# Second attention layer: the residual added by an accumulating DMA, more rows normalised by ScalarE

## The chip, the cores and the metric

The kernel runs on one NeuronCore of a Trainium2 chip. The engines work side by side, each through its own instructions in program order, and wait for one another through semaphores: TensorE (PE) multiplies matrices into PSUM, VectorE (DVE) and ScalarE (ACT) work element by element, GpSimd (POOL) does the rest, and SyncE (SP) issues transfers. The metric is the device time of one execution in microseconds; the kernel before takes 428.71 us (median of 3 runs, 428.61 to 428.74).

## The reference

Four residual layers run one after the other on x with 2048 positions of 512 features in bf16: attention, convolution, attention, convolution. The change touches the second attention.

```python
def _layernorm(x, axis=-1, eps=1e-5):
    m = jnp.mean(x, axis=axis, keepdims=True)
    v = jnp.var(x, axis=axis, keepdims=True)
    return (x - m) / jnp.sqrt(v + eps)

def _A_ref(x, wqkv, wo):          # 32 heads of 16; window W = 8 keys, dilation 2
    ...
    logits = jnp.einsum("bhsd,bhswd->bhsw", q, kg) * scale
    attn = _softmax(logits, axis=-1)
    o = jnp.einsum("bhsw,bhswd->bhsd", attn, vg)
    return o.transpose(...).reshape(B, S, D) @ wo

x = x + _A_ref(_layernorm(x), A_wqkv, A_wo)
x = x + _B_ref(_layernorm(x), ...)      # long convolution by way of the FFT
x = x + _A_ref(_layernorm(x), A_wqkv, A_wo)   # the layer of the change
x = x + _B_ref(_layernorm(x), ...)
```

So after the attention each position needs x plus the projected output, and then the mean and variance of this sum over 512 features, for the normalisation ahead of the last layer.

## The kernel before

The position s is 16*p + a: p is the partition, a is one of 16 "rows", each a tile of 128 partitions by 512 features. x lives in SBUF as `x_sb[128, 16, 512]`, bf16. The attention's second half is a loop of 16 iterations n, over the rows in the order 0, 2, 1, 3, 4, ... 15. What each engine does in it:

```python
def pv_mult(n):                       # VectorE: attention weights times the 8 values
    nc.vector.tensor_tensor(pv[:], attn..., vap, ALU.mult)          # L404, tile pav, 128x4096
def pv_sum(n):                        # TensorE: sum over the window and transpose
    ... 32 matmuls of pav by ident into po                          # L412
    nc.scalar.copy(oT[:], po[:])                                    # L415

def out_proj(a):                      # TensorE: residual and projection in one PSUM tile
    oT = oTs.pop(a)
    pw = pq_tile()
    xr = x_sb[:, a, :]
    nc.tensor.matmul(pw[:], lhsT=ident[:], rhs=xr, start=True, stop=False)                    # L422
    for ftp in range(NDT):
        nc.tensor.matmul(pw[:], lhsT=oT[:, ftp, :], rhs=self.wo[:, ftp, :], start=False, ...) # L424
    if a >= 12:
        if a >= 14 and l == 1:
            row_stats(nc, lnst, pw[:], a, "dve")
        nc.scalar.copy(xr, pw[:])                                                             # L428
    else:
        nc.scalar.activation(xr, pw[:], ACT.Identity, accum_out=lnst["s1"][:, a:a + 1])       # L430
        row_sumsq(nc, lnst, xr, a)                 # ScalarE: Square, summed into s2            L108
```

The loop, in program order (l is 1 in the second attention layer; parts for the softmax of later rows are cut):

```python
for n in range(16):
    pv_mult(rows[n])
    ...                                      # n = 0, 8: mx; n = 2, 10: recip; n = 4, 11: norm_p
    if n in (1, 3, 5, 7):
        mult(3, n // 2)                      # VectorE, last products of queries and keys
    if n in (7, 11, 15):
        u_begin(n - 7, n - 3, "act", "act" if n > 7 else "pool")
    if n in (8, 12):
        u_end(n - 8)                         # VectorE: bias nb = -mean * rstd                  L148
    if n in (9, 10, 13, 14):
        b0 = 0 if n < 11 else 4
        r0 = b0 + (0 if n in (9, 13) else 2)
        u_apply(b0, range(r0, r0 + 2))       # even rows ScalarE (L158), odd rows VectorE (L160)
    if n == 15:
        x_stats(12)                          # VectorE: bn_stats of a row                       L101
    ...
    pv_sum(rows[n])
    if n == 15:
        x_stats(13)
        u_end(8)
        u_apply(8, range(8, 12), "dve")
    if n > 0:
        out_proj(rows[n - 1])
    ...
u_begin(12, 15, "dve", "act"); out_proj(15)
self.warm(pw, 10, ...)                       # ten matmuls that keep TensorE busy
u_begin(15, 16, "dve", "act"); u_end(12); ...  # rows 12 to 15 normalised, the next layer begins
```

`u_begin` of four rows turns their sums into the reciprocal standard deviation:

```python
mean, ms = lnst["s1"][:, a0:a1], -1.0 / D
nc.vector.scalar_tensor_tensor(msq[:], mean, -1.0 / (D * D), mean, ALU.mult, ALU.mult)              # L133
nc.vector.scalar_tensor_tensor(veps[:], lnst["s2"][:, a0:a1], 1.0 / D, msq[:], ALU.mult, ALU.add)   # L135
if rs == "act":
    return rstd_act(...)                     # ScalarE: Ln with bias EPS (L118), then Exp (L119)
nc.vector.tensor_scalar(rstd[:], var, EPS, None, ALU.add)                # L140
nc.gpsimd.tensor_tensor(rstd[:], rstd[:], lnst["mh"][:, 0:n], ALU.pow)   # L141
```

The tiles `pav`, `oT`, `po` and `pq` have two buffers each. At the front of this layer the mean and variance of x are already computed once, for the normalisation ahead of it (`bn_aggr` into a tile `agg[b]`).

Of the kernel before, what the change touches and what calls it, by code (L numbers as in the profile page):

```python
# [10 lines left out]
ACT = mybir.ActivationFunctionType  # L11
ALU = mybir.AluOpType
AX = mybir.AxisListType
PSUM = bass.MemoryType.PSUM
F32 = mybir.dt.float32
BF16 = mybir.dt.bfloat16
# [4 lines left out]
P = 128  # L21
S = 2048
D = 512
# [3 lines left out]
NA = 16  # L27
NDT = 4
# [70 lines left out]
def row_stats(nc, lnst, x_row, a, eng):  # L99
    if eng == "dve":  # L100
        nc.vector.bn_stats(lnst["bn"][:, a, 0, :], x_row)  # L101
    else:
        nc.scalar.activation(lnst["junk"][:], x_row, ACT.Identity, accum_out=lnst["s1"][:, a:a + 1])
        row_sumsq(nc, lnst, x_row, a)


def row_sumsq(nc, lnst, x_row, a):
    nc.scalar.activation(lnst["junk"][:], x_row, ACT.Square, accum_out=lnst["s2"][:, a:a + 1])  # L108
# [7 lines left out]
def rstd_act(nc, pool, var):  # L116
    rstd = pool.tile(list(var.shape), F32, name="ln_rstd")
    nc.scalar.activation(rstd[:], var, ACT.Ln, bias=EPS)  # L118
    nc.scalar.activation(rstd[:], rstd[:], ACT.Exp, scale=-0.5)  # L119
    return rstd  # L120


def ln_begin(nc, pool, lnst, a0, a1, eng, rs="pool"):
    n = a1 - a0
    if eng == "dve":
        ag = pool.tile([P, n, 2], F32, name="ln_ag")
        for a in range(n):
            nc.vector.bn_aggr(ag[:, a, :], lnst["bn"][:, a0 + a, 0, :])
        var, mean, ms = ag[:, :, 1], ag[:, :, 0], -1.0
    else:  # L130
        mean, ms = lnst["s1"][:, a0:a1], -1.0 / D
        msq = pool.tile([P, n], F32, name="ln_msq")
        nc.vector.scalar_tensor_tensor(msq[:], mean, -1.0 / (D * D), mean, ALU.mult, ALU.mult)  # L133
        veps = pool.tile([P, n], F32, name="ln_veps")
        nc.vector.scalar_tensor_tensor(veps[:], lnst["s2"][:, a0:a1], 1.0 / D, msq[:], ALU.mult, ALU.add)  # L135
        var = veps[:]
    if rs == "act":
        return rstd_act(nc, pool, var), mean, ms
    rstd = pool.tile([P, n], F32, name="ln_rstd")
    nc.vector.tensor_scalar(rstd[:], var, EPS, None, ALU.add)  # L140
    nc.gpsimd.tensor_tensor(rstd[:], rstd[:], lnst["mh"][:, 0:n], ALU.pow)  # L141
    return rstd, mean, ms
# [20 lines left out]
class LayerA:  # L163
# [143 lines left out]
    def core(self, x_sb, u, lnp, ev=None, nprod=0):  # L307

        tc, nc, lnst, l = self.tc, self.nc, self.lnst, self.layer
        ident, nident = self.c["ident"], self.c["nident"]  # L310
# [11 lines left out]
        with ExitStack() as c2:  # L322
# [7 lines left out]
            wk = c2.enter_context(tc.tile_pool(name=f"a{l}_wk", bufs=2, reuse_waits="tile"))  # L330
# [9 lines left out]
            def pq_tile():  # L340
                return ps_q.tile([P, 512], F32, name="pq", tag="pq")
# [76 lines left out]
            def out_proj(a):  # L418
                oT = oTs.pop(a)
                pw = pq_tile()  # L420
                xr = x_sb[:, a, :]
                nc.tensor.matmul(pw[:], lhsT=ident[:], rhs=xr, start=True, stop=False)  # L422
                for ftp in range(NDT):
                    nc.tensor.matmul(pw[:], lhsT=oT[:, ftp, :], rhs=self.wo[:, ftp, :], start=False, stop=(ftp == NDT - 1))  # L424
                if a >= 12:
                    if a >= 14 and l == 1:
                        row_stats(nc, lnst, pw[:], a, "dve")
                    nc.scalar.copy(xr, pw[:])  # L428
                else:
                    nc.scalar.activation(xr, pw[:], ACT.Identity, accum_out=lnst["s1"][:, a:a + 1])  # L430
                    row_sumsq(nc, lnst, xr, a)

            def x_stats(a):
                row_stats(nc, lnst, x_sb[:, a, :], a, "dve")

            def u_begin(a0, a1, eng, rs="pool"):
                lns[a0] = ln_begin(nc, lnp, lnst, a0, a1, eng, rs)
# [11 lines left out]
            def u_end(a0):  # L449
                lns[a0] = ln_end(nc, lnp, lns[a0])  # L450

            def u_apply(a0, rows, eng=None):
                rstd, nb = lns[a0]
                for a in rows:
                    ln_apply(nc, u[:, :, a, :], x_sb[:, a, :].rearrange("p (q r) -> p q r", r=4), rstd, nb, a - a0,
                             eng or ("dve" if a % 2 else "act"))
# [45 lines left out]
            rows = [0, 2, 1, *range(3, NA)]  # L502
            for n in range(16):
                pv_mult(rows[n])
                if n in (0, 8):
                    mx(2 + n // 8)
                if n in (2, 10):
                    recip(2 + n // 8)
                if n in (4, 11):
                    norm_p(2 + n // 8)  # L510
                if n in (1, 3, 5, 7):
                    mult(3, n // 2)
                if n in (7, 11, 15):
                    u_begin(n - 7, n - 3, "act", "act" if n > 7 else "pool")
                if n in (8, 12):
                    u_end(n - 8)
                if n in (9, 10, 13, 14):
                    b0 = 0 if n < 11 else 4
                    r0 = b0 + (0 if n in (9, 13) else 2)
                    u_apply(b0, range(r0, r0 + 2))  # L520
                if n == 15:
                    x_stats(12)
                event(("p", n))
                if n in (1, 3, 5):
                    q_proj(3, n // 2 + 1)
                pv_sum(rows[n])
                if n in (0, 8):
                    sub_exp(2 + n // 8)
                if n == 15:
                    x_stats(13)  # L530
                    if l == 1:
                        u_end(8)
                        u_apply(8, range(8, 12), "dve")
                if n > 0:
                    out_proj(rows[n - 1])
                if n in (1, 3, 5, 7):
                    lsum(3, n // 2)
                event(("o", n))
# [7 lines left out]
            pw = pq_tile()  # L546
# [729 lines left out]
def kernel(  # L1276
# [16 lines left out]
    nc = tc.nc  # L1293
# [6 lines left out]
    with tc.tile_pool(name="ctmp", bufs=1) as tmp:  # L1300
        consts = build_a_consts(tc, nc, cpool, tmp)
    lnst = dict(s1=cpool.tile([P, NA], F32, name="ln_s1"), s2=cpool.tile([P, NA], F32, name="ln_s2"),
                bn=cpool.tile([P, NA, 2, 6], F32, name="ln_bn"), junk=cpool.tile([P, D], BF16, name="ln_junk"),
                mh=cpool.tile([P, 4], F32, name="ln_mh"))
# [12 lines left out]
    xpool = ctx.enter_context(tc.tile_pool(name="xres", bufs=1))  # L1317
    lnp = ctx.enter_context(tc.tile_pool(name="ln_small", bufs=3, reuse_waits="tile"))
    lnst["bn"] = xpool.tile([P, NA, 2, 6], F32, name="ln_bn2")
    x_sb = xpool.tile([P, NA, D], BF16, name="x_sb")  # L1320
# [56 lines left out]
    with tc.manual_schedule(engines=MAN):  # L1377
        la.front_open()
        ln, agg, pts = {}, {}, {}

        def front_pools():
            fb.swap_psum()
            la.front_psum()

        def aggr(b):
            agg[b] = lnp.tile([P, 4, 2], F32, name="ln_ag")
            for a in range(4):
                nc.vector.bn_aggr(agg[b][:, a, :], lnst["bn"][:, 4 * b + a, :, :])

        def power(b):  # L1390
            ln[b] = rstd_act(nc, lnp, agg[b][:, :, 1]), agg[b][:, :, 0], -1.0

        def norm(b):
            la.front_apply(b, x_sb[:, b * 4:(b + 1) * 4, :], ln_end(nc, lnp, ln[b]), ["dve"] * 4)

        def transposes(b):
            pts[b] = la.front_t(b)

        def last(*ops):
            def f():  # L1400
                for op, *ix in ops:
                    front[op](*ix)
            return f

        front = dict(S=front_pools, h=lambda g, t: half_stats(nc, lnst, x_sb, t, g), a=aggr, p=power, n=norm, T=transposes,
                     E=lambda b, d, eng: pts[b][d](eng), P=lambda b, ft: la.front_k(b, ["act"] * 4, (ft,)),
                     Q=lambda q, ft: la.qproj1(q, ft, la.qT[q], la.ps_pj, la.pj_tag), x=lambda b: la.front_ext(b, "dve"),
                     e=lambda ft: la.front_ext(3, "dve", ft))
        fb.run(ORDERF, None, more=front)
        la.front_close()  # L1410
        fb.c_ps.close()
        fb.c_grp.close()
        krctx.close()
        ev = {("p", 8): [lambda: la.load_w2(w2_dram)]}
        ev["m", 0, 0] = [last(("P", 3, 0), ("P", 3, 1), ("x", 0), ("x", 2), ("P", 3, 2), ("Q", 0, 1), ("e", 0), ("Q", 0, 2))]
        ev["m", 0, 1] = [last(("e", 1), ("e", 2))]
        ev["m", 0, 2] = [last(("e", 3))]
        ev["q", 0, 0] = [last(("P", 3, 3), ("Q", 0, 3))]
        la.core(x_sb, u, lnp, ev)
# [51 lines left out]
```

## Time and profile before

| what | value |
|---|---|
| time | 428.71 us |
| span of the profiled execution | 426.7 us |
| VectorE products `pav`, one | 2.284 us, 32 in the kernel, 16 in this layer |
| row loop of the second attention | VectorE's first `pav` at 314.9 us, its last from 364.96 us |
| statistics and bias of the last rows | 367.2 to 374.6 us |
| first TensorE step of the last layer | 375.3 us |

In the profile, L-numbers are lines of the kernel. A line of the timeline has the start in us from the span's start, the duration, the engine, line and operation, the tile written and those read, and in brackets how long the engine sat idle before it and for whom. Times of instructions overlap a little, because an engine takes up the next before the last has drained; so the cost of an instruction in a full stretch is the step from its start to the next start. A view of stretches gives the busy time of each engine between two times.

### The profile page before, as it was taken

To read this page: it belongs to the slowest core of one execution; us is meant where nothing else is said; L and a number is where in the kernel's file an instruction comes from. 1 tells how busy PE (TensorE), PEld (TensorE's weight loads), DVE (VectorE), ACT (ScalarE), POOL (GpSimd) and SP (SyncE) were. 2 spreads that over 40 slices of the span, in tenths; PEclk is the share of its full clock that TensorE was granted. 3 is DMA by queue.
4 is the path that set the end of the run, shared out by engine and by line. 5 is a ranking of instruction groups with operands and counts; after the bars stand their busy time and mean duration, and the time that the engine had idled before them with its cause. 6 is when DMAs were issued, how large, how long until landed. Compare 5 with 4: busy or idle time off the path is not lost.

```text
span 426.7 us, 12737 instructions
## 1 busy us (share of the span) xinstructions
PE 354.2 (83%) x5506; PEld 265.2 (62%) x5506; DVE 395.0 (93%) x537; ACT 323.1 (76%) x554; POOL 43.9 (10%) x46
## 2 busy tenths in 40 slices
PE   3000169999999899999998999999998999997894
PEld 2000127667765687767887898555566777776793
DVE  8999999999999999996999949899999999889864
ACT  6999999986455389887999988755556668689961
POOL 3000300000598000001300000000000020000000
PEclk9999998999999899999999999999999999999999
DMA  8930732132116743572244692810141066416315
GB/s 217 395 103 12 82 78 69 33 68 59 24 40 188 245 109 102 178 298 102 76 175 177 222 322 59 261 56 2 38 111 28 2 229 224 141 55 181 118 40 160
DMA packets 62466, 54.16 MB, mean 127 GB/s; under 512 B 33893, under 2 KB 50890, under 8 KB 61130
## 3 DMA queue, kind: packets, MB, share of 16 engines
q1 hardware_dynamic: 62266, 53.22, 40.6%
q8 instruction: 43, 0.70, 0.8%
q10 hardware_dynamic: 144, 0.13, 0.3%
q14 instruction: 13, 0.11, 0.1%
HBM read 30.28 MB, written 13.24 MB: 102 GB/s over the span
## 4 chain that ended last, share of the span: by engine, by line
PE 46%; DVE 22%; ACT 7%; DMA 4%; issue 3%; SPq 2%; DVEq 0%; ACTq 0%
PE po L412 9%; DVE t L805 5%; DVE pav L404 5%; PE pq L351 4%; PE pk L1165 4%; PE pq L424 4%; DVE a1s L745 4%; PE pp L1103 4%; PE L L302 4%; DVE prod L295 3%; PE pp L242 3%; PE pq L185 3%; PE pb L831 2%; PE pb L832 2%; DMA kf_ring<-kf_dram 1%
## 5 line engine op out<-in xcount | busy, mean ns | idle before, releaser
L404 DVE TENSOR_TENSOR pav<-attn,v_ext 128x4096 bf16<-128x4096 bf16 x32 | 73.0, 2283 | 0.4 <-DMA v_ext<-v_ext 0.4
L412 PEld LDWEIGHTS <-pav 128*128 128x128 bf16 x1024 | 60.0, 99 | 11.1 <-DVE pav L404 7.5
L412 PE MATMUL po<-ident,pav 128*128 128x128 bf16 x1024 | 64.0, 222 | 3.1 <-DVE pav L404 2.8
L295 DVE TENSOR_TENSOR prod<-qT,kT_ext 128x4096 bf16<-128x4096 bf16 x29 | 66.4, 2308 | 0.2
L1093 PE MATMUL pt<-ident,x_blk 128*128 128x128 bf16 x64 | 6.7, 258 | 43.2 <-ACT x_blk L158 43.2
L1005 DVE TENSOR_TENSOR A_t<-A_t,pow_t 128x1024 bf16<-128x1024 bf16 (+4 forms) x46 | 38.3, 873 | 0.2
L1093 PEld LDWEIGHTS <-x_blk 128*128 128x128 bf16 x64 | 5.5, 119 | 46.0 <-ACT x_blk L158 44.0
L818 ACT CAST ub<-pb 128x1024 bf16<-128x1024 f32 x32 | 32.5, 1062 | 1.3 <-DVE t L805 1.1
L353 ACT CAST v_ext<-pq 128x512 bf16<-128x512 f32 x32 | 18.7, 586 | 19.3 <-PE pq L351 18.1
L424 PE MATMUL pq<-wop,oT 128*128 128x512 bf16 x128 | 32.9, 379 | 0.0
L302 PEld LDWEIGHTS <-prod 128*128 128x128 bf16 x928 | 27.1, 96 | 8.8 <-DVE prod L295 3.2
L415 ACT CAST oT<-po 128x512 bf16<-128x512 f32 x32 | 18.5, 579 | 18.2 <-PE po L412 18.0
L1103 PE MATMUL pp<-xnT,kT_ext 128*128 128x512 bf16 x96 | 27.9, 421 | 4.5 <-ACT qT L1108 2.6
L831 PE MATMUL pb<-Wp,t 128*128 128x128 bf16 x256 | 30.2, 219 | 1.8 <-ACT ub L818 0.8
L763 PE MATMUL pb<-a1s,w_sb 128*128 128x64 bf16 x768 | 27.7, 193 | 4.8 <-ACT ub L818 3.5
L351 PE MATMUL pq<-wv,xnT 128*128 128x512 bf16 x128 | 30.7, 379 | 0.0
L745 DVE CAST a1s<-pb 128x1024 bf16<-128x1024 f32 x22 | 26.1, 1217 | 4.9 <-PE pb L756 4.8
L832 PE MATMUL pb<-WpJ,t 128*128 128x128 bf16 x256 | 30.0, 219 | 0.4 <-DVE t L805 0.4
L763 PEld LDWEIGHTS <-w_sb 128*128 128x128 bf16 x768 | 24.8, 98 | 7.5 <-issue 5.9
L302 PE MATMUL L<-ind,prod 128*128 128x8 bf16 x928 | 27.4, 166 | 1.3 <-DVE prod L295 1.1
L745 ACT CAST a1s<-pb 128x1024 bf16<-128x1024 f32 x26 | 25.6, 1043 | 2.0 <-PE pb L756 2.0
L832 PEld LDWEIGHTS <-t 128*128 128x128 bf16 x256 | 24.9, 98 | 3.0 <-issue 1.6
(227 smaller groups left out, 861.1 us busy)
## 6 DMA issues: line engine op xcount, KB each, us to landing
w_sb<-w_dram SPq DMA_DIRECT2D x8, 1024.0 KB, 8.3
w_dram<-w_zero SPq DMA_DIRECT2D x1, 4096.0 KB, 15.5
kf_ring<-kf_dram SPq DMA_DIRECT2D x13, 256.0 KB, 3.6
kf_ring<-kf_dram SPq DMA_DIRECT2D x26, 128.0 KB, 3.6
v_ext<-v_ext SPq DMA_DIRECT2D x4, 784.0 KB, 6.6
x_blk<-in_A_x_dram SPq DMA_DIRECT2D x4, 512.0 KB, 4.1
kT_ext<-in_A_wqkv_dram SPq DMA_DIRECT2D x4, 512.0 KB, 10.8
x_sb<-in_A_x_dram SPq DMA_DIRECT2D x4, 512.0 KB, 4.9
```

Of the source, the lines that this page charges most:

```text
L295: nc.vector.tensor_tensor(pr, self.qT[q][:, ft].unsqueeze(1).to_broadcast([P, W, 4, P]), kap, ALU.mult)
L302: self.nc.tensor.matmul(L[:, al, w, ft * 8:(ft + 1) * 8], lhsT=pr[:, w, al, :], rhs=self.c["ind8"][:], start=(ft == 0 and w == 0 and al % ...
L351: nc.tensor.matmul(pp[:], lhsT=xnT[:, dt, a * P:(a + 1) * P], rhs=wv[:, dt, :], start=(dt == 0), stop=(dt == NDT - 1))
L404: nc.vector.tensor_tensor(pv[:], attn[:, n % 4].unsqueeze(2).to_broadcast([P, W, DH, H]), vap, ALU.mult)
L412: nc.tensor.matmul(po[:, ft, :], lhsT=pvf[:, w, ft * P:(ft + 1) * P], rhs=ident[:], start=(w == 0 and ft == 0), stop=(w == W - 1), skip_gr ...
L424: nc.tensor.matmul(pw[:], lhsT=oT[:, ftp, :], rhs=self.wo[:, ftp, :], start=False, stop=(ftp == NDT - 1))
L745: (self.nc.scalar.copy if eng == "act" else self.nc.vector.tensor_copy)(dst, src)
L763: nc.tensor.matmul(p2[:, j, :], lhsT=self.w2[:, ec * EC + j, :], rhs=a1s[:, ec * EC + j, :], start=True, stop=True)
L831: nc.tensor.matmul(p3[:, j, :], lhsT=t1[:, dql, :], rhs=wp_r, start=True, stop=False)
L832: nc.tensor.matmul(p3[:, j, :], lhsT=t2[:, dql, :], rhs=wpj_r, start=False, stop=True)
L1005: return lambda: nc.vector.tensor_tensor(*args)
L1103: nc.tensor.matmul(pps[kind, b, ft][:], lhsT=la.wqk[:, dt, c:c + P], rhs=la.xnT[:, dt, b * 512:(b + 1) * 512], start=(dt == 0), stop=(dt = ...
```

## The change

For rows 0 to 11 of the second attention layer, the residual is no longer added by TensorE. ScalarE moves the projected output from PSUM to a bf16 tile `ow` of two buffers and sums it on the way, and GpSimd's queue adds `ow` to the row of `x_sb` in a DMA. The sum of squares reads the row after that, so it is taken two iterations later. The sum of a row is now that of the output plus 512 times the old mean of x, which is kept from the front of the layer in `mean0`. Rows 1, 3, 5 and 7 are normalised by ScalarE, no longer by VectorE, and the first `u_begin` takes its power by ScalarE's Ln and Exp instead of GpSimd. The purpose is to take work from TensorE and VectorE and to use GpSimd's queue, which is free.

```diff
@@ ln_begin
         mean, ms = lnst["s1"][:, a0:a1], -1.0 / D
+        if "mean0" in lnst:
+            nc.vector.scalar_tensor_tensor(mean, lnst["mean0"][:, a0:a1, 0], float(D), mean, ALU.mult, ALU.add)
         msq = pool.tile([P, n], F32, name="ln_msq")
@@ out_proj
-                nc.tensor.matmul(pw[:], lhsT=ident[:], rhs=xr, start=True, stop=False)
+                by_dma = l == 1 and a < 12
+                if not by_dma:
+                    nc.tensor.matmul(pw[:], lhsT=ident[:], rhs=xr, start=True, stop=False)
                 for ftp in range(NDT):
-                    nc.tensor.matmul(pw[:], lhsT=oT[:, ftp, :], rhs=self.wo[:, ftp, :], start=False, stop=(ftp == NDT - 1))
-                if a >= 12:
+                    nc.tensor.matmul(pw[:], lhsT=oT[:, ftp, :], rhs=self.wo[:, ftp, :],
+                                     start=(by_dma and ftp == 0), stop=(ftp == NDT - 1))
+                if by_dma:
+                    ow = wk.tile([P, D], BF16, name="ow")
+                    nc.scalar.activation(ow[:], pw[:], ACT.Identity, accum_out=lnst["s1"][:, a:a + 1])
+                    nc.gpsimd.dma_start(xr, ow[:], accum_op=ALU.add)
+                elif a >= 12:
@@ the loop
                 if n in (7, 11, 15):
-                    u_begin(n - 7, n - 3, "act", "act" if n > 7 else "pool")
+                    u_begin(n - 7, n - 3, "act", "act" if n > 7 or l else "pool")
...
-                    u_apply(b0, range(r0, r0 + 2))
+                    u_apply(b0, range(r0, r0 + 2), "act" if l else None)
...
                 if n > 0:
                     out_proj(rows[n - 1])
+                if l == 1 and 3 <= n < 15:
+                    row_sumsq(nc, lnst, x_sb[:, rows[n - 3], :], rows[n - 3])
@@ the front of the second attention layer
+        mean0 = xpool.tile([P, NA, 2], F32, name="ln_mean0")
...
-            agg[b] = lnp.tile([P, 4, 2], F32, name="ln_ag")
+            agg[b] = mean0[:, 4 * b:4 * b + 4, :]
...
+        lnst["mean0"] = mean0
```

## The prediction

> **What bounds the kernel now.** I began with the page's table of busy time by engine.
>
> ```profile
> PE 354.2 (83%) x5506; PEld 265.2 (62%) x5506; DVE 395.0 (93%) x537; ACT 323.1 (76%) x554; POOL 43.9 (10%) x46
> ```
>
> VectorE leads, but the change touches one stage only, the row loop of the second attention layer. By the timeline its first attention product `pav` starts at 314.9 us and the next layer's first TensorE step at 375.3. So I cut that stage into stretches (columns: stretch, its length, then busy us and count of PE, PEld, DVE, ACT, POOL, then clock, DMA share, GB/s).
>
> ```profile
> 323.00:347.00 24.00, 22.88 (x361) 17.97 (x359) 23.74 (x17) 14.29 (x37) 1.73 (x1) 1.00 0.06 14
> 347.00:357.00 10.00, 9.75 (x122) 7.11 (x120) 9.90 (x12) 7.90 (x19) 1.16 (x1) 1.00 0.93 392
> 357.00:371.00 14.00, 13.97 (x183) 11.02 (x183) 12.61 (x18) 10.09 (x26) 0.00 (x0) 1.00 0.37 115
> ```
>
> VectorE fills the first two stretches, TensorE the third, and ScalarE has room on average (14.3 of 24 us, 7.9 of 10, 10.1 of 14). An average hides bursts, so next I read ScalarE's timeline for iterations n = 10 and 11 (columns: start, duration, instruction, idle before it).
>
> ```profile
> 353.94 0.60 ACT L430 ACTIVATE x_sb<-pq 128x512 bf16<-128x512 f32 x1 [0.47 <-PE pq L424]
> 354.44 0.20 ACT L430 ACTIVATION_READ_ACCUMULATOR x_sb<-pq 128x1 f32 x1
> 354.66 0.63 ACT L108 ACTIVATE ln_junk<-x_sb 128x512 bf16<-128x512 bf16 x1
> ...
> 355.83 0.80 ACT L158 ACTIVATE xnT<-x_sb,ln_nb,ln_rstd 128x512 bf16<-128x512 bf16 x1
> 356.54 0.56 ACT L415 CAST oT<-po 128x512 bf16<-128x512 f32 x1
> 357.00 0.59 ACT L430 ACTIVATE x_sb<-pq 128x512 bf16<-128x512 f32 x1
> 357.49 0.20 ACT L430 ACTIVATION_READ_ACCUMULATOR x_sb<-pq 128x1 f32 x1
> 357.72 0.63 ACT L108 ACTIVATE ln_junk<-x_sb 128x512 bf16<-128x512 bf16 x1
> 358.26 0.19 ACT L108 ACTIVATION_READ_ACCUMULATOR ln_junk<-x_sb 128x1 f32 x1
> ```
>
> The reader is to see that ScalarE runs back to back through n = 10 (only 0.47 us idle before n = 9's eviction), and that L108, the sum of squares that follows the eviction of row 9, ends only at 358.45. Steps from start to start: eviction 0.72, sum of squares 0.63, one normalised row 0.71, `oT` 0.46. VectorE at the same time, and at the loop's end:
>
> ```profile
> 357.37 0.15 DVE L133 SCALAR_TENSOR_TENSOR ln_msq<-ln_s 128x4 f32<-128x4 f32 x1
> 357.56 0.16 DVE L135 SCALAR_TENSOR_TENSOR ln_veps<-ln_s,ln_msq 128x4 f32<-128x4 f32 x1
> 357.64 2.28 DVE L404 TENSOR_TENSOR pav<-attn,v_ext 128x4096 bf16<-128x4096 bf16 x1
> ...
> 367.42 0.16 DVE L135 SCALAR_TENSOR_TENSOR ln_veps<-ln_s,ln_msq 128x4 f32<-128x4 f32 x1
> 367.50 0.69 DVE L101 BATCH_NORM_STATS2 ln_bn<-x_sb 128x6 f32<-128x512 bf16 x1
> 369.40 0.69 DVE L101 BATCH_NORM_STATS2 ln_bn<-x_sb 128x6 f32<-128x512 bf16 x1 [1.22 <-ACT x_sb L428]
> ```
>
> L135 (`veps`) reads the sums of squares of four rows, and stands in VectorE's order ahead of the next `pav`. It now waits for nothing, because its rows were squared two iterations earlier. At the end, row 12's and row 13's statistics follow it.
>
> **What the Trainium skill says.** "DMA: Bandwidth & Descriptors", section "SWDGE vs HWDGE vs iDMA": accumulating in a DMA can only be issued from GpSimd; this case's queues of before are hardware and instruction queues only, so the trace has no such transfer. The section "Anatomy of one DMA — SWDGE (gpsimd) path" of the same page fits 2.0 us plus bytes over 436 GB/s; for a row of 128 KB that is an estimate of 2.3 us, to which reading the destination adds something it doesn't give. "SBUF — State Buffer", section "Who interferes with whom": a VectorE operation with two SBUF inputs holds GpSimd's reads out, but, inferred there, not the writing of descriptors. The first half agrees with the trace: GpSimd's power of 4 columns took 2.89 us from 345.27, through the `pav` of 345.00 and into the reduction of 347.31. The second half nothing here shows.
>
> **The change part by part.** (1) TensorE loses one identity matmul for each of 12 rows. In the timeline L422 starts at 361.77 and L424 at 361.99, so 0.22 us each, 2.6 in all; but until 357 TensorE follows `pav`, so only those of its late, full stretch could count. (2) VectorE loses four normalised rows in n = 9, 10, 13, 14, at 0.33 us from start to start (350.73 to 351.05), 1.3 in all, and gains three operations of four columns at 0.19, 0.6 in all, of which one takes the place of adding epsilon at n = 7. (3) ScalarE gains four normalised rows, 4 x 0.71 = 2.8 us, two each in n = 9 to 10 and 13 to 14, plus Ln and Exp at n = 7. (4) The sum of squares of row n-3 now runs after row n-1's eviction, two iterations later than before, so that the DMA has time; its consumer `veps` stays where it was. This is what decides, I think.
>
> First I follow the chain to n = 11. Nothing in VectorE's order changes up to 348.5. At n = 7 `veps` needs row 3, squared at n = 6, about 344.5 by the same steps: just in time. ScalarE from n = 8: `oT` 349.3, the exponential 349.8 (1.03), eviction of row 7 350.8, squares of row 5 351.5, two normalised rows from 352.2, `oT` 353.6, eviction of row 8 354.0, squares of row 6 354.75, Ln and Exp of the reciprocal 355.4, two rows from 355.9, `oT` 357.3, eviction of row 9 357.8, squares of row 7 from 358.5 to 359.25. VectorE, relieved of two rows, would have `veps` of rows 4 to 7 at 357.56 - 0.66 + 0.19 = 357.1; it has to wait until 359.3. The `pav` of n = 12 starts at 359.4 instead of 357.64, **1.75 us late**. Even in ScalarE's old pace its slot ends at 358.45, so a delay of about 0.9 is certain in this order.
>
> Then to the end. `pav` of n = 12 ends at 361.6; TensorE takes 1.79 us for each row's `po` sum and 0.86 (rows below 12) or 1.08 for the projection. ScalarE: evicts row 11 at 364.5, squares row 9 365.2, two rows from 365.85, `oT` 367.25, copies row 12 367.7 (0.5), squares row 10 368.2, two rows from 368.9, `oT` 370.3, copies row 13 370.75, squares row 11 371.25 to 371.98. TensorE alone would give row 13 at 370.0 and so the squares at 371.5. Only then can `veps` of rows 8 to 11 run, at 372.03, and in VectorE's order rows 12 and 13 follow: statistics at 372.11 and 372.73, the latter against 369.40 before. What comes after it keeps its length: bias, four normalised rows, statistics of row 14, its copy, ten warming matmuls, the first step of the next layer. The stage ends **3.3 us later** (372.73 - 369.40). From there VectorE and ScalarE are busy nearly throughout (13.4 and 13.5 of 14 us from 376 to 390), so I carry the shift whole: 428.71 + 3.3 = 432.0 us.
>
> **Rivals.** *TensorE and VectorE are relieved, and it pays.* If the squares came in time, `pav` of n = 12 would start 0.47 us earlier (0.66 less 0.19), and TensorE, full from there, would save one more identity matmul: about 0.7 us, 428.0 us. For it speak the full engines of the stretches; against it that ScalarE, which takes up the work, has no gaps left exactly in n = 9 to 10. *The transfer becomes the wait.* On my chain row 7 is evicted by 351.5 and squared at 358.5, row 8 354.7 and 361.2; the eviction of row 9 into the two-buffer tile needs row 7's transfer 6.3 us after issue. So 6 us are hidden, against an estimated 2.3 plus something. The stretch 347 to 357 moves 392 GB/s for the next layer's weights at a DMA share of 0.93, and there it might take 5 to 7 us; at 8 us each wait adds up to 2 us, 434 to 436. *GpSimd's issue slows VectorE* through shared access: the same DMA page, section "Latency and other measured facts", gives about 1 us from a GpSimd issue to the first byte, so 12 issues could cost some 10 us as an estimate, 440 us; in the trace all 32 `pav` take 2.27 to 2.29 us, also the one beside GpSimd's power, which speaks against it.
>
> **Range and chances.** The delay at n = 11 is fixed by program order, and TensorE's floor keeps most of it to the end, 2.8 us. A slip of some steps gives 429.6 below; transfers that hold ScalarE up give 435.0 above. Over 2% is 8.6 us, which only the third rival reaches. I predict **432.0 us, 429.6 to 435.0**, chances 0.01 faster, 0.93 within 2%, 0.06 slower.
>
> **What would show it.** Right: in VectorE's timeline an idle time of about 2 us before the second `veps`, released by ScalarE's L108-type squares, and a larger one, some 3.5 us, before the third; ScalarE without gaps from 350 to 360; transfers landing within 6 us; `pav` still at 2.28 us. Wrong: `veps` without a wait; squares that start on a DMA's arrival; a first TensorE step of the next layer before 375; or a later stage that gives back the shift.

## The result, and the profile after

The changed kernel takes **436.01 us** (median of 4 runs, 435.42 to 436.29) against 428.66 of the kernel before: a ratio of 1.0173, 95% interval 1.0156 to 1.0191, 7.35 us slower. The prediction was 432.0 us, 429.6 to 435.0. So the direction was right, but the predicted loss, 3.3 us, is less than half of the measured one.

The same views as before. First busy time by engine from the page, and the new queue among the DMA queues (packets, MB, share of the DMA engines' time):

```profile
PE 352.2 (81%) x5494; PEld 264.8 (61%) x5494; DVE 393.9 (91%) x535; ACT 324.5 (75%) x560; POOL 51.6 (12%) x57
...
q0 software_dynamic: 1728, 1.57, 2.4%
```

TensorE and VectorE do less work than before, as intended (2.0 and 1.1 us), and the kernel is slower: the loss is all waiting. Here is the row loop in stretches, moved by about 1 us, with the same columns as in the prediction (clock, DMA share and GB/s are the last three):

```profile
324.00:348.00 24.00, 22.35 (x359) 17.71 (x356) 23.79 (x18) 13.49 (x36) 5.37 (x6) 1.00 0.26 40
348.00:358.00 10.00, 9.38 (x123) 7.30 (x124) 9.39 (x10) 7.02 (x18) 2.59 (x3) 1.00 1.03 388
358.00:379.00 21.00, 15.86 (x178) 12.25 (x176) 12.09 (x17) 13.71 (x34) 2.59 (x3) 0.92 0.49 130
```

Up to 348 nothing is lost. The third stretch, in which TensorE was full for 14.0 us, is now 21 us long, no engine fills it, and TensorE's granted clock falls to 0.92. VectorE's timeline shows for what it waited:

```profile
358.55 0.16 DVE L135 SCALAR_TENSOR_TENSOR ln_msq<-ln_s 128x4 f32<-128x4 f32 x1
362.98 0.16 DVE L137 SCALAR_TENSOR_TENSOR ln_veps<-ln_s,ln_msq 128x4 f32<-128x4 f32 x1 [4.27 <-ACT ln_junk L108]
...
368.85 2.29 DVE L406 TENSOR_TENSOR pav<-attn,v_ext 128x4096 bf16<-128x4096 bf16 x1 [1.23 <-PE po L414]
...
377.01 0.16 DVE L137 SCALAR_TENSOR_TENSOR ln_veps<-ln_s,ln_msq 128x4 f32<-128x4 f32 x1 [2.95 <-ACT ln_junk L108]
```

`veps` of rows 4 to 7 waits 4.27 us for the squares of row 7, that of rows 8 to 11 2.95 us for those of row 11, as the prediction said of both; but the first wait was to be 2.2 us and the second the longer one, some 3.5, and that a `pav` waits for TensorE was not in it. ScalarE's timeline tells why the squares were so late:

```profile
355.88 0.60 ACT L432 ACTIVATE ow<-pq 128x512 bf16<-128x512 f32 x1 [0.84 <-DMA x_sb<-ow]
...
361.65 0.60 ACT L432 ACTIVATE ow<-pq 128x512 bf16<-128x512 f32 x1 [2.06 <-DMA x_sb<-ow]
362.14 0.19 ACT L432 ACTIVATION_READ_ACCUMULATOR ow<-pq 128x1 f32 x1
362.24 0.62 ACT L108 ACTIVATE ln_junk<-x_sb 128x512 bf16<-128x512 bf16 x1
```

The evictions of rows 8 and 9 find both `ow` buffers taken, since rows 6 and 7 have not landed in `x_sb`; the squares of row 7 (362.24) stand behind the second. The DMA view, taken around each issue, gives the time from issue to landing of each addition:

| row | 0 | 2, 1, 3, 4 | 5 | 6 | 7 | 8 | 9 | 10 | 11 |
|---|---|---|---|---|---|---|---|---|---|
| issued at, us | 326.0 | 330.4 to 341.5 | 345.2 | 348.0 | 352.85 | 357.1 | 362.9 | 365.2 | 370.9 |
| us to landing | 4.5 | 2.6 to 2.7 | 5.2 | 7.8 | **8.7** | 5.0 | 4.0 | 4.4 | 2.8 |

Row 7 lands at 361.6, and at once the eviction of row 9 starts. Rows 5 to 8 share the DMA engines with the next layer's weights, issued from 345.8 on, rows 9 and 10 with its filters, issued from 361.4 on. Row 6 already waits for its first packet: issued at 348.04, it has none from 350 to 352 (the additions' queue moves nothing in these 2 us, and 89 packets in the next 2), so it starts about 4 us after its issue, where rows 1 to 5 took 1.4. GpSimd's part is short meanwhile: it needs 0.86 us for an issue, beside `pav` of unchanged length.

```profile
352.85 0.86 POOL L433 DMA_DIRECT2D x_sb<-ow  x1 [3.94 <-ACT ow L432]
357.09 0.86 POOL L433 DMA_DIRECT2D x_sb<-ow  x1 [3.38 <-ACT ow L432]
```

The last new thing is TensorE's. Its `po` sum for n = 12, from its timeline, and its clock from the view of stretches (third number from the end):

```profile
365.40 3.41 PE L414 MATMUL po<-ident,pav 128*128 128x128 bf16 x32 [4.71 <-DVE pav L406]
```

```profile
362.00:364.00 2.00, 0.00 (x0) 0.00 (x0) 1.02 (x2) 1.74 (x8) 0.86 (x1) 1.00 0.59 167
364.00:366.00 2.00, 0.60 (x6) 0.60 (x7) 2.00 (x3) 1.29 (x5) 0.79 (x1) 0.77 0.86 220
366.00:368.00 2.00, 2.00 (x22) 2.00 (x20) 1.62 (x1) 0.00 (x0) 0.07 (x1) 0.50 0.81 296
368.00:370.00 2.00, 2.00 (x23) 1.53 (x21) 1.15 (x1) 0.88 (x2) 0.00 (x0) 0.88 0.85 235
```

Near the end of 4.71 us without work TensorE's clock falls to half, for about 3.4 us, and the sum takes 3.41 us against 1.96 in the same view before.

### The profile page after: what moved, and what is told of

The parts are those of the page before. It is cut to its first block, busy times and chain, and to the rows that moved or that the text cites. A ratio compares the mean times of both kernels' runs of the same rounds, so it can differ in the third digit from the quotient of the medians.

```text
span 434.4 us, 12772 instructions
## 1 busy us (share of the span) xinstructions
PE 352.2 (81%) x5494; PEld 264.8 (61%) x5494; DVE 393.9 (91%) x535; ACT 324.5 (75%) x560; POOL 51.6 (12%) x57
## 4 chain that ended last, share of the span: by engine, by line
PE 42%; DVE 15%; ACT 11%; issue 8%; DMA 7%; POOL 1%; SPq 1%; DVEq 0%; ACTq 0%; POOLq 0%
PE po L414 5%; PE pk L1176 5%; PE pq L353 4%; PE pp L1114 4%; DVE pav L406 4%; DVE prod L297 3%; PE pp L244 3%; PE L L304 3%; PE pq L187 3%; PE pb L842 2%; PE pb L843 2%; ACT ub L829 2%; DMA x_sb<-ow 2%; PE pq L428 2%; PE pb L774 2%
## 5 line engine op out<-in xcount | busy, mean ns | idle before, releaser
L414 PE MATMUL po<-ident,pav 128*128 128x128 bf16 x1024 | 65.5, 225 | 8.6 <-DVE pav L406 8.4
L414 PEld LDWEIGHTS <-pav 128*128 128x128 bf16 x1024 | 61.4, 101 | 16.6 <-DVE pav L406 13.0
L297 DVE TENSOR_TENSOR prod<-qT,kT_ext 128x4096 bf16<-128x4096 bf16 x29 | 66.3, 2307 | 0.2
L1114 PE MATMUL pp<-xnT,kT_ext 128*128 128x512 bf16 x96 | 27.0, 409 | 5.4 <-ACT qT L1119 2.5
```

The lines of the kernel that those rows point to most:

```text
L297: nc.vector.tensor_tensor(pr, self.qT[q][:, ft].unsqueeze(1).to_broadcast([P, W, 4, P]), kap, ALU.mult)
L414: nc.tensor.matmul(po[:, ft, :], lhsT=pvf[:, w, ft * P:(ft + 1) * P], rhs=ident[:], start=(w == 0 and ft == 0), stop=(w == W - 1), skip_gr ...
L1114: nc.tensor.matmul(pps[kind, b, ft][:], lhsT=la.wqk[:, dt, c:c + P], rhs=la.xnT[:, dt, b * 512:(b + 1) * 512], start=(dt == 0), stop=(dt = ...
```

## The experiments

**Theory A** is the prediction's: the squares, two iterations late, stand behind `veps` in time. **Theory B**: the additions land too late behind the weights. **Theory C**: TensorE's clock falls during the wait. All are edits of the changed kernel. Profiled executions differ by up to 1.6 us already ahead of n = 8 (`veps` of rows 0 to 3 lies between 344.60 and 346.18, in no relation to the edits; in the changed kernel 1.1 us are a wait for a transfer at 245 us, in the layer before). So besides the time I give the length of the stage: from the start of `pav` of n = 8 to the first TensorE step of the last layer. Before:

```profile
345.00 2.28 DVE L404 TENSOR_TENSOR pav<-attn,v_ext 128x4096 bf16<-128x4096 bf16 x1
375.27 0.24 PE L756 MATMUL pb<-F1c,xnT 128*64 128x128 bf16 x1
```

and in the changed kernel:

```profile
346.13 2.28 DVE L406 TENSOR_TENSOR pav<-attn,v_ext 128x4096 bf16<-128x4096 bf16 x1
383.38 0.24 PE L767 MATMUL pb<-F1c,xnT 128*64 128x128 bf16 x1
```

The kernel with rows on ScalarE only has 29.95 us in both of its profiles. The one with the weights "at n = 12" is in effect the changed kernel again, and its stage differs from that by 0.55 us; so smaller differences between kernels with early weights decide nothing.

| kernel | time, us | ratio to before, 95% interval | stage, us |
|---|---|---|---|
| before | 428.66 | 1 | 30.27 |
| changed | 436.01 | 1.0173 (1.0156 to 1.0191) | 37.25 |
| residual on TensorE, squares late | 432.00 | 1.0068 (1.0048 to 1.0088) | 33.10 |
| rows on ScalarE only | 428.06 | 0.9986 (0.9977 to 0.9996) | 29.95 |
| DMA, odd rows on VectorE | 435.69 | 1.0158 (1.0137 to 1.0180) | 37.38 |
| weights "at n = 12" | 436.09 | 1.0168 (1.0146 to 1.0189) | 37.80 |
| weights after row 11 | 432.53 | 1.0079 (1.0056 to 1.0101) | 32.69 |
| warming matmuls | 434.44 | 1.0125 (1.0082 to 1.0168) | 35.36 |
| four `ow` buffers | 434.56 | 1.0134 (1.0093 to 1.0176) | 36.37 |
| weights in 16 pieces | 434.26 | 1.0135 (1.0093 to 1.0178) | 35.99 |
| order and weights mended | 428.97 | 1.0009 (1.0001 to 1.0018) | 30.48 |
| order alone mended | 430.96 | 1.0052 (1.0034 to 1.0069) | 32.88 |
| rows on ScalarE only, again | 427.88 | 0.9984 (0.9978 to 0.9991) | 29.95 |

### The order alone

```diff
-                by_dma = l == 1 and a < 12
+                by_dma = False
...
                     nc.scalar.activation(xr, pw[:], ACT.Identity, accum_out=lnst["s1"][:, a:a + 1])
-                    row_sumsq(nc, lnst, xr, a)
+                    if l == 0:
+                        row_sumsq(nc, lnst, xr, a)
```

(`mean0` is not handed on, since the sum has the residual in it.)

> The residual goes back to TensorE (no transfer, no ow tile); the late squares and the eight rows on ScalarE stay. Theory A (program order: the squares come two iterations late and ScalarE has no room, so VectorE waits at veps): 431.5 to 432.5 us, veps of rows 4 to 7 about 1.8 us late and those of rows 8 to 11 about 3.3 us late, as the chain of the prediction has it. Theory B (the transfers behind the weights are the whole cause): 428 to 429 us, no wait at veps above 1 us.

432.00 us, and both waits where theory A has them. VectorE's timeline:

```profile
358.68 0.16 DVE L137 SCALAR_TENSOR_TENSOR ln_veps<-ln_s,ln_msq 128x4 f32<-128x4 f32 x1 [2.02 <-ACT ln_junk L108]
...
371.48 0.16 DVE L137 SCALAR_TENSOR_TENSOR ln_veps<-ln_s,ln_msq 128x4 f32<-128x4 f32 x1 [3.14 <-ACT ln_junk L108]
```

There is no transfer in it, so late squares, with the rows on ScalarE, cost 432.00 - 428.76 = 3.2 us (428.76 is the kernel before on that chip). B as the whole cause has fallen, but 4 us of the loss remain for what the transfers bring.

### The rows on ScalarE alone

```diff
-                by_dma = l == 1 and a < 12
+                by_dma = False
...
-                if l == 1 and 3 <= n < 15:
-                    row_sumsq(nc, lnst, x_sb[:, rows[n - 3], :], rows[n - 3])
```

(`mean0` again is not handed on.)

> Only the normalised rows 1, 3, 5, 7 on ScalarE and the first rstd by Ln and Exp; residual on TensorE and squares at once, as before. Theory A: the rows alone don't hurt, as the squares of rows 4 to 7 are long there: 427.9 to 428.9 us, perhaps 0.7 us gained because pav of n = 12 starts 0.66 us earlier. A third theory, that ScalarE is simply overloaded by 2.8 us of rows, would make it 430 to 431.5 us.

428.06 us, slightly faster than before, and again so in a second run:

> The rows-on-ScalarE kernel once more, beside the two above on the same chip, to settle whether it beats the kernel before: 427.7 to 428.4 us against 428.3 to 428.8, a ratio of 0.998 to 0.999 with an interval below 1.

427.88 us, ratio 0.9984 (0.9978 to 0.9991). With the squares taken at once, `veps` of rows 4 to 7 waits for nothing:

```profile
358.37 0.16 DVE L137 SCALAR_TENSOR_TENSOR ln_veps<-ln_s,ln_msq 128x4 f32<-128x4 f32 x1
```

This version beats the kernel before by 0.6 to 0.7 us. The stage shows 0.3 of it (30.27 - 29.95); where the rest arises isn't shown. ScalarE's load alone isn't the cause of the loss. The kernel above differs from this one only by the late squares, which so cost 432.00 - 428.06 = 3.9 us. Whether they would cost less with the odd rows left on VectorE was not run without transfers.

### The transfers without the extra rows

```diff
-                    u_apply(b0, range(r0, r0 + 2), "act" if l else None)
+                    u_apply(b0, range(r0, r0 + 2))
```

> Residual by DMA and late squares, but the odd rows stay on VectorE. Theory A without transfers: veps of rows 4 to 7 about 0.9 to 1.2 us late, 430.5 to 431.5 us. Theory B: row 7 lands only after the weights, some 8.7 us after its issue, the squares of row 7 wait for it or for the ow buffer behind it, veps is 4 us late again, 435 to 436.5 us, near the changed kernel.

435.69 us, as B has it, and not told apart from the changed kernel. The VectorE line:

```profile
361.15 0.16 DVE L137 SCALAR_TENSOR_TENSOR ln_veps<-ln_s,ln_msq 128x4 f32<-128x4 f32 x1 [3.82 <-ACT ln_junk L108]
```

Two normalised rows less for ScalarE in n = 9 and 10 win nothing, since it then waits for row 7 longer (3.7 us for `ow` in all, against 2.9).

### The weights later: an edit that did nothing, and one that did

```diff
-        ev = {("p", 8): [lambda: la.load_w2(w2_dram)]}
+        ev = {("p", 12): [lambda: la.load_w2(w2_dram)]}
```

> The changed kernel with the 4 MB load of the next layer's weights issued at n = 12 instead of n = 8. Theory A alone: transfers land in about 3 us, no wait for ow, but the order stays: 431.5 to 432.5 us. Theory B alone: 428 to 429 us. Clock theory: TensorE's wait for pav shrinks from 4.7 to about 2.5 us and its po sums stay at 1.8 us instead of 3.4.

436.09 us, nothing changed, and this is no verdict. SyncE's line gives the reason:

```profile
345.22 2.22 SPq L571 DMA_DIRECT2D w_sb<-w_dram  x4
```

SyncE issues nothing else between, so its order doesn't say when this goes out. The weights take the buffer of the keys, which VectorE's last `prod` reads until 345.1 (L297), and for this alone SyncE waits, as before the edit. To hold it back takes something to wait for:

```diff
+        scr = xpool.tile([1, 64], BF16, name="scr")
-        ev = {("p", 8): [lambda: la.load_w2(w2_dram)]}
+        ev = {("p", 13): [lambda: nc.sync.dma_start(scr[:], x_sb[0:1, 11, 0:64]), lambda: la.load_w2(w2_dram)]}
```

> The changed kernel, but the 4 MB weights load is held back by a 128-byte transfer that reads row 11 after its addition, so it starts after the last accumulating transfer (at about 368 us). If the transfers behind the weights make the second half of the loss: additions land in about 3 us, no wait for ow, TensorE waits some 2 us at n = 12 and keeps its clock: 431.5 to 433 us, as with the residual on TensorE. If the accumulating DMA costs by itself (GpSimd, memory, a slow add), it stays at 435 to 436.5. Above that, if the weights now come too late for the next layer (needed near 385 us).

432.53 us. The weights now start at 368.9:

```profile
368.89 2.12 SPq L571 DMA_DIRECT2D w_sb<-w_dram  x4
```

All rows but the first land in 2.6 to 3.0 us, and no eviction waits for `ow`. (The filters behind the weights in SyncE's order move too, from 361.4 to 382.0; for rows 9 and 10 the two are not told apart.) What is left are the order's two waits, nearly those of the kernel without transfers:

```profile
358.73 0.16 DVE L137 SCALAR_TENSOR_TENSOR ln_veps<-ln_s,ln_msq 128x4 f32<-128x4 f32 x1 [1.80 <-ACT ln_junk L108]
...
371.31 0.16 DVE L137 SCALAR_TENSOR_TENSOR ln_veps<-ln_s,ln_msq 128x4 f32<-128x4 f32 x1 [2.95 <-ACT ln_junk L108]
```

So no cost of the accumulating DMA by itself is seen here, and the meeting with the bulk loads, with all that follows from it, costs the other half: 37.25 - 32.69 = 4.6 us of the stage.

### TensorE's clock

```diff
                 event(("p", n))
+                if l == 1 and n == 12:
+                    self.warm(pq_tile(), 12, self.wo[:, 0, :])
```

> The changed kernel with 12 warming matmuls (2.6 us at full clock) on TensorE ahead of row 12's po sum, so that it idles some 2 us in two pieces instead of 4.7 us. Clock theory: the po sum takes 1.8 us again instead of 3.4 and the next pav don't wait for it, 434.3 to 435 us, about 1.4 us less. If the slow sum has another cause: 435.8 to 436.5.

434.44 us, the stage 1.9 us shorter. TensorE's timeline:

```profile
362.06 2.75 PE L213 MATMUL pq<-wop,ident 128*128 128x512 bf16 x11 [1.36 <-ACT ow L432]
365.08 1.96 PE L414 MATMUL po<-ident,pav 128*128 128x128 bf16 x32 [0.26 <-DVE pav L406]
```

The sum takes 1.96 us again, and the clock stays at 1.00 in every 2 us from 360 to 372. `veps` still waits 3.93 us (row 7 landed after 8.3 us, not 8.7). From there to the end of the stage it takes 381.60 - 362.65 = 18.95 us, the changed kernel 383.38 - 362.98 = 20.40. So C is a cause of its own that the long wait sets off, worth 1.5 of the 1.9 us; the rest lies ahead of `veps`. By the times alone the intervals overlap; the sum's length and the clock are what shows it.

### Buffers and pieces

```diff
-                    ow = wk.tile([P, D], BF16, name="ow")
+                    ow = wk.tile([P, D], BF16, name="ow", bufs=4)
```

> The changed kernel with four buffers for ow instead of two. If the loss is in the buffers: the evictions of rows 8 and 9 no longer wait (0.84 and 2.06 us) and about 3 us come back, 433 us. If it is in the landing of row 7, which its squares need: the wait moves from the eviction to the squares of row 7, veps of rows 4 to 7 still comes near 362.3, and the time is 435 to 436.

434.56 us, between the two. The wait moved, as the second alternative said. ScalarE:

```profile
361.33 0.63 ACT L108 ACTIVATE ln_junk<-x_sb 128x512 bf16<-128x512 bf16 x1 [1.74 <-DMA x_sb<-ow]
```

The eviction of row 9 is free now (358.9), but the squares of row 7 need row 7 itself. The eviction no longer stands behind the wait, and the stage is 0.9 us shorter, little more than the 0.55 us by which two profiles of the changed kernel differ; the interval overlaps that of the changed kernel. `veps` still waits 3.88 us: the landing, not the buffer, holds it up.

```diff
-        for c in range(4):
-            self.nc.sync.dma_start(self.w2[:, c * 32:(c + 1) * 32, :], ...)
+        k = 16 if self.layer else 4
+        n = 128 // k
+        for c in range(k):
+            self.nc.sync.dma_start(self.w2[:, c * n:(c + 1) * n, :], ...)
```

> The changed kernel with the weights load in 16 transfers (2 KB a partition each) instead of 4 (8 KB a partition). If an addition's pieces take turns with the weights' pieces, so that each waits for a long one: rows 5 to 8 land within 3 to 5 us instead of 5.0 to 8.7, the evictions wait little, and the time is 431.5 to 433.5 us. If an addition waits until the weights queued ahead of it have gone: rows 5 to 8 land as late as now, 435.5 to 436.5 us.

434.26 us; rows 5 to 8 land in 3.9, 7.2, 7.3 and 6.6 us. Neither expectation holds: rows 6 and 7 gain 0.6 and 1.4 us, row 8, which met the longer issue of 16 transfers (11.6 us of SyncE), loses 1.6, and the interval again overlaps that of the changed kernel. Row 6 has its first packet 3.4 us after its issue, against 4.0: so smaller pieces of the weights don't take away this wait ahead of the first packet. What an addition waits for there stays open.

### Both mended

Row 11 stays with TensorE and is squared at once; `u_begin` of rows 4 to 7 moves behind the squares of row 7; the weights wait for row 10.

```diff
-                by_dma = l == 1 and a < 12
+                by_dma = l == 1 and a < 11
...
-                if n in (7, 11, 15):
-                    u_begin(n - 7, n - 3, "act", "act" if n > 7 or l else "pool")
-                if n in (8, 12):
-                    u_end(n - 8)
+                if n in ((7, 12, 15) if l else (7, 11, 15)):
+                    b = {7: 0, 11: 4, 12: 4, 15: 8}[n]
+                    u_begin(b, b + 4, "act", "act" if n > 7 or l else "pool")
+                if n in ((8, 13) if l else (8, 12)):
+                    u_end(0 if n == 8 else 4)
...
-                if l == 1 and 3 <= n < 15:
+                if l == 1 and 3 <= n < 14:
...
+        ev = {("p", 12): [lambda: nc.sync.dma_start(scr[:], x_sb[0:1, 10, 0:64]), lambda: la.load_w2(w2_dram)]}
```

(The `mean0` correction covers rows below 11.)

> Both repairs: residual by DMA for rows 0 to 10, row 11 by TensorE with its squares at once; u_begin of rows 4 to 7 one iteration later (n = 12), after the squares of row 7; weights held until row 10 has landed. If order and landing are the whole cause, no veps waits over 0.3 us and the time is that of the rows-on-ScalarE kernel, 427.9 to 428.7 us: the eleven matmuls taken from TensorE bring nothing more, since TensorE waits for pav up to n = 12 anyway. If the DMA costs something else by itself: 429.5 us or more. If the matmuls do count: 427 us or less.

428.97 us: 6.9 of the 7.35 us are gone, though not all as expected. VectorE:

```profile
359.77 0.16 DVE L139 SCALAR_TENSOR_TENSOR ln_veps<-ln_s,ln_msq 128x4 f32<-128x4 f32 x1
...
367.74 0.16 DVE L139 SCALAR_TENSOR_TENSOR ln_veps<-ln_s,ln_msq 128x4 f32<-128x4 f32 x1 [0.79 <-ACT ln_junk L108]
```

The first wait is gone; the second `veps` waits 0.79 us, more than the 0.3 I allowed, for row 10's squares, late at n = 13 by the same order. It is 0.5 us behind the kernel with rows on ScalarE only by the stage (30.48 - 29.95), 1.1 us by time. The eleven matmuls taken from TensorE show no gain.

> The same with the weights issued as in the changed kernel. Row 7 and row 8 land 8 and 5 us after issue again; ScalarE stops at the eviction behind row 7 until about 361.5, and veps of rows 4 to 7, now at n = 12, comes near 362.5 instead of 359.3: about 3 us lost, 430.5 to 432.5 us. If order alone was the cause: 428 to 429.

The same with the weights issued early: 430.96 us, 2 us above the mended one. `veps` and, ahead of it, ScalarE's eviction of row 9:

```profile
361.49 0.17 DVE L139 SCALAR_TENSOR_TENSOR ln_veps<-ln_s,ln_msq 128x4 f32<-128x4 f32 x1 [1.22 <-ACT ln_junk L108]
```

```profile
360.16 0.60 ACT L434 ACTIVATE ow<-pq 128x512 bf16<-128x512 f32 x1 [1.40 <-DMA x_sb<-ow]
```

With the order mended the late landing costs 2 us by time, not 4. `veps` comes an iteration later, so less of the wait is left, and the clock holds: no pause of TensorE is longer than 0.82 us from 345 to 372, and the clock is 1.00 in every 2 us from 354 to 374.

## Why the prediction was wrong, by its steps

**What bounds the loop** held: `pav` first (VectorE busy 23.79 of 24.00 us up to 348), and the work taken away from the engines was not what set the time.

**The order step** held, and nearly in size: in the kernel without transfers the wait of 2.2 us measures 2.02, the stage's 3.3 us 2.8. That its time is the predicted 432.0 to the hundredth is luck, since it keeps the twelve identity matmuls that the chain leaves out. The chain's own case is the changed kernel with the weights held back, 432.53 us.

**The step that failed** is the second rival's "So 6 us are hidden". The hidden time was reckoned well: the evictions of rows 8 and 9 stood ready 7.0 and 6.7 us after the issue of rows 6 and 7 (355.88 - 0.84 - 348.04, and 361.65 - 2.06 - 352.85). The landing was mis-sized: an estimated 2.3 us and something, "5 to 7 us" behind the weights; measured 2.6 to 3.0 alone and 7.8 and 8.7 for rows 6 and 7 behind them. The stretch with the DMA share of 0.93 was in view, and I put the case among the rivals, at 434 to 436 us, instead of into the sum. That the time came out at the edge of that range is partly luck: the rival had only the waits for `ow`, up to 2 us each (measured 0.84 and 2.06), and not the clock.

**The term that was missing** is in "TensorE takes 1.79 us for each row's po sum": the sum for n = 12 took 3.41 us in the profile and 1.96 with the clock held (1.79 is from start to start; 1.96 goes to the end of the last matmul, as it did before). I had let VectorE's wait grow and not asked what an idle TensorE does. The Trainium skill's page "TensorE: Matmul & The Clock Gate", section "Part 1: The HAM clock gate", says that after an idle window of about 3.4 us the clock falls to half, and that these windows run free of the kernel. The runs agree in that the half clock lasts 3.4 or 6.8 us and isn't tied to the start of the pause, and differ in that it fell 2.3 us after the last matmul in one of them, as listed at the end.

**The sum**, by the stage, whose +6.98 us are nearly the whole +7.35: order 2.4 (weights held back, 32.69 - 30.27; 2.8 without transfers), late landing 3.1 (from the stage's start to `veps` of rows 4 to 7 the changed kernel takes 16.85 us, with the weights held back 13.75), and clock 1.5 (from there on 20.40 against 18.94, and 18.95 with the warming matmuls). In the profile with the weights "at n = 12" the last two are 2.6 and 2.5, so they are good to half a microsecond or one. The three aren't independent: with the order mended, the late landing costs 2.4 (32.88 - 30.48) at full clock.

**The other rivals.** That the relief pays is true of the rows that left VectorE, 0.6 to 0.7 us by time; of the matmuls nothing is seen. That GpSimd's issue slows VectorE has fallen: every `pav` of the stage takes 2.28 or 2.29 us in the changed kernel, also under an issue, and an issue takes 0.86 us, which bears out what the Trainium skill's page "SBUF — State Buffer", section "Who interferes with whom", infers on descriptors. The first packet of an addition that met nothing came 1.4 us after its issue began, not about 1. And no later stage gave the shift back.

## What to carry to other kernels

Moving an operation from a busy engine to a transfer moves its consumers in program order too; look for the instruction of the full engine that reads the late result, and for which of its neighbours has to move with it. A short transfer's time is that of the stretch it meets, so measure it beside the bulk load that shares the DMA engines, not alone; and give the bulk load something to wait for, since its place in an otherwise empty queue doesn't delay it. Before trusting a predicted wait, ask what the engine behind it loses by standing still.

## What the hardware showed that I had not expected

- An addition of 128 KB in SBUF, issued from GpSimd, lands 2.6 to 3.0 us after its issue when alone (the first one took 3.1 to 4.7), whereof GpSimd is busy 0.86; behind a 4 MB load at some 390 GB/s it took up to 8.7 us.
- TensorE's clock, cut into quarters of a microsecond, did not follow the length of the pause before `po` of n = 12:

| kernel | pause, us | clock fell, us after the last matmul | half clock, us | the sum, us |
|---|---|---|---|---|
| DMA, odd rows on VectorE | 4.23 | 2.3 | 6.8 | 3.60 |
| weights "at n = 12" | 4.13 | 2.5 | 6.8 | 3.60 |
| changed | 4.71 | 4.4 | 3.4 | 3.41 |
| weights in 16 pieces | 3.82 | 4.4 | 3.4 | 3.06 |
| four `ow` buffers | 4.29 | 5.3 | 3.4 | 2.72 |

In the last two TensorE had been back at work at full clock for 0.6 and 1.0 us when it fell. After pauses of 1.67 us (no transfers) and 2.22 us (weights after row 11) it did not fall. Nothing between 2.2 and 3.8 us was measured, so these runs give no threshold.
